# Replacing a list scheduler by a written-out order table in a fused linear-attention and mixture-of-experts kernel

## The chip, the cores and the metric

The kernel runs on one core of a Trainium2 chip. The metric is the device time of one execution in microseconds. The kernel before takes 152.34 us (median of three runs, 151.07 to 153.26).

## What is computed

The first half is a linear attention with a decaying state, for 4 sequences of 768 tokens and 8 heads of 48 channels; the second sends each whole sequence through one of 8 experts, chosen by the mean of the attention's output.

```python
# attention, per sequence b and head h; state is 48x48
for t in range(S):
    y[t]  = r[t] @ (state + outer(u * k[t], v[t]))
    state = w[:, None] * state + outer(k[t], v[t])
# mixture of experts: x = y of all heads side by side, [768, 384]
logits = x.mean(axis=0) @ w_gate            # 8 logits for the sequence
e      = argmax(logits)
out    = softmax(logits)[e] * (relu(x @ w1[e]) @ w2[e])   # 384 -> 1024 -> 384
```

Inputs and outputs are float32; the matrix products of the kernel are in bf16, except the gate's.

## The kernel before

**Blocks.** The 3072 tokens are cut into 12 blocks of 256 tokens (`g`, three to a sequence). A block has two halves of 128 rows, `j` being a half of the partitions and `c` the parity of the token. For each block the kernel

- loads k, r and v (`load`, L71 to L80, 384 KB each, on the sync queue);
- scales k and r by powers of the decay and casts them (`scale`, L362; GpSimd, 1.82 us a piece), and casts v (`prep_v`, L373; ScalarE);
- turns k and r by TensorE (`transposes`, L377, the tile `twp`) and takes them out of PSUM (`evac_t`, the tile `kr`);
- forms products for the bonus term u (`prod`, `bonus`, `bonus_out`, `bonus_v`: tiles `prod`, `tcol`, `vt`);
- multiplies scores k times r in two rounds (`scores`, tile `at`, always the same PSUM bank pair), and masks them on VectorE (`masked`, tile `gt`, 1.22 us);
- multiplies masked scores by v into two banks (`y_mms`), adds the part of the carried state (`inter`) and of the bonus (`add_bonus`, step name `vt y`), and updates the state (`state_mms`, `state_out`, `carried`, PSUM tile `s`);
- casts the result to bf16 (`evac_y`, tile `xn`), adds up its columns for the mean (`pool_mms`), and turns it back to channels by tokens (`turn_back`, `evac_x`, tile `xt`).

**Sequences.** After three blocks come the sum of the pool (`pool_sum`), the gate's logits (`gate`, tile `lgp`), the choice (`choose`, maximum and its index on VectorE), and `weights` (L635): GpSimd reads the expert's number into a register and issues three transfers of that expert's weights, which convert to bf16 on the way. Then follow 16 up-projection steps of three matmuls (`mm1`, tile `hp`), each with a rectified evacuation (`relu`, tile `ht`), and 6 down-projection tiles in two halves of four matmuls each (`mm2`, tile `op`), each with a multiplication by the gate's weight (`gated`, tile `ob`) and then a store.

**Order.** [...] Each piece is a *step* with the engines that may do it and an estimated duration on each, the steps that it needs, the PSUM banks that it uses, and whether it takes or frees one of three rotating banks (`b0` to `b2`). `schedule` (L234) is a list scheduler over these: it keeps an estimated clock per engine, and takes the ready step that could start first, among equals the one with the longest tail of work plus a hand-set lead (`LEAD`, L216). If its estimate leaves TensorE a gap of over 0.35 us it fills it with matmuls on zeros (`fill`, L110), which are there to keep TensorE active.

**Buffers and waits around the change.** The loaded k, r and v have four buffers each (`AHEAD = 4`, L49), so the load of block g waits until block g - 4 has been scaled and cast. From block 6 on (`FENCED = 6`, L847) the loads also stand behind `fence`, a four-byte transfer on the same sync queue that waits for the gate's weight of sequence 0 and comes after the first expert's weights have been issued. The gate's logits take one of the three rotating banks from `gate` to `exp`.

Of the kernel before, what the change touches and what calls it, by code (L numbers as in the profile page):

```python
# [14 lines left out]
ACT = mybir.ActivationFunctionType  # L15


@with_exitstack
def kernel(
# [29 lines left out]
    AHEAD = 4  # L49
# [4 lines left out]
    xpool = ctx.enter_context(tc.tile_pool(name="xpool", bufs=B))  # L54
# [33 lines left out]
    wrow = const.tile([1, DM], FP32, tag="wrow", name="wrow")  # L88
# [17 lines left out]
    nc.sync.dma_start(out=wg, in_=moe_w_gate.rearrange("(p ct) e -> p ct e", p=128))  # L106
# [12 lines left out]
    fill("b0", 5)  # L119
# [24 lines left out]
    lnw = const.tile([128, H, D], FP32, tag="lnw", name="lnw")  # L144
# [51 lines left out]

    class Step:
        def __init__(self, key, on, emit, needs, banks, takes, frees, form, lands):
            self.key, self.on, self.emit, self.needs = key, on, emit, list(needs)
            self.banks, self.takes, self.frees = list(banks), takes, frees  # L200
            self.form, self.lands = form, lands
            self.then, self.tail, self.scale = [], 0.0, 1.0

    steps = {}
    lands = {}

    def step(key, on, emit, needs=(), banks=(), takes=None, frees=None, form=None, data=()):
        assert key not in steps, key
        steps[key] = Step(key, on, emit, [n for n in needs if n is not None], banks, takes,
                          frees, form, list(data))  # L210

    ANY = ("b0", "b1", "b2")
    FORM = 0.1
    RUN = 3
    SCALE0, SCALE = 4.35, 3.77
    LEAD = {  # L216
        "weights": 20.0, "gate sums": 20.0, "gate": 29.7, "choose": 24.1, "mm2": -1.8,
        "r": -2.7, "v": -1.6, "load": 12.4, "mm1": 2.4, "t": 0.5, "tcol": 3.8, "carry": -1.1,
        "relu": -4.2, "late": -1.0, "kr": -2.7, "y": 4.8, "xn": -7.6, "gated": 8.4, "gt": -1.3,
        "vt y": 2.3,  # L220
    }
    names = {"PE": nc.tensor, "DVE": nc.vector, "ACT": nc.scalar, "POOL": nc.gpsimd,
             "SP": nc.sync}

    def lag(src, dst, settled):
        if src == dst:
            return 0.0
        if src == "PE":
            return 0.22
        if dst == "PE":  # L230
            return 0.1 if settled else 0.3
        return 0.15

    def schedule(free, lands_first, chains):  # L234
        lands.update(lands_first)
        for s in steps.values():
            for n in s.needs:
                steps[n].then.append(s.key)
        links = {}
        for chain in chains:  # L240
            for x, y in zip(chain, chain[1:]):
                links.setdefault(x, []).append(y)
        done = set()

        def tail(key):
            stack = [key]
            while stack:
                x = stack[-1]
                if x in done:
                    stack.pop()  # L250
                    continue
                after = steps[x].then + links.get(x, [])
                rest = [y for y in after if y not in done]
                if rest:
                    stack.extend(rest)
                    continue
                s = steps[x]
                s.tail = s.scale * min(s.on.values()) + max(
                    [steps[y].tail for y in after], default=0.0)
                done.add(x)  # L260
                stack.pop()

        for key in steps:
            tail(key)

        end, eng_of = {}, {}
        bank_use = {}
        owner = dict.fromkeys(ANY)
        held = {}
        open_at = dict.fromkeys(ANY, 0.0)  # L270
        form, stream = ["128"], [0.0]
        left = {k: len(s.needs) for k, s in steps.items()}
        ready = [k for k, n in left.items() if n == 0]
        settled = [True]

        def start_on(s, e):
            t = free[e]
            for n in s.needs:
                t = max(t, end[n] + lag(eng_of[n], e, settled[0]))
            for x in s.lands:  # L280
                t = max(t, lands[x])
            for bank in s.banks:
                for other, till in bank_use.get(bank, {}).items():
                    if other != e:
                        t = max(t, till + lag(other, e, settled[0]))
            if s.takes:
                spare = [open_at[x] for x in ANY if owner[x] is None]
                if not spare:
                    return None
                t = max(t, min(spare))  # L290
            return t

        while ready:
            best = {}
            for k in ready:
                s = steps[k]
                if any(x not in lands for x in s.lands):
                    continue
                for e in s.on:
                    t = start_on(s, e)  # L300
                    if t is not None:
                        best.setdefault(e, []).append((t, k))
# [47 lines left out]
            for n in s.then:  # L350
                left[n] -= 1
                if left[n] == 0:
                    ready.append(n)
# [544 lines left out]
```

## Time and profile before

| | us |
|---|---|
| median of three runs | 152.34 |
| span of the profiled execution | 150.4 |
| TensorE busy | 133.4 (89%) |
| VectorE busy | 73.4 (49%) |
| ScalarE busy | 83.8 (56%) |
| GpSimd busy | 67.9 (45%) |
| up-projection matmuls (`hp`), 192 | 35.6 |
| down-projection matmuls (`op`), 192 | 34.7 |
| mask products (`gt`), 24 | 29.2, 1.22 each |
| k and r scalings on GpSimd, 22 | 40.1, 1.82 each |

TensorE's mean granted clock is 0.932 of full. A line of the page's groups gives the source line, the engine, the operation with the program's names for output and input, the number of instructions, busy time and mean of one, and the engine's idle time just before them with what ended it. [...] The chain of work is followed back from the last instruction, at each step to whatever released it. Times in the trace count from the start of the span. Line numbers are those of the kernel before.

### The profile page before, as it was taken

How to read it: one execution, taken by the hardware profiler on the slowest of the kernel's cores; microseconds unless marked ns; L12 is line 12 of the kernel's file. 1: busy time of each engine (PE TensorE's matmuls, PEld its weight loads, DVE VectorE, ACT ScalarE, POOL GpSimd, SP SyncE). 2: the span in 40 equal slices, each digit the busy share in tenths (PEclk: the TensorE clock that was granted, in tenths of full speed). 3: DMA queues.
4: the chain of work that ended last, by engine and by line, in shares of the span. 5: the costliest groups of instructions: out<-in, count | busy, mean ns of one | idle time of the engine just before them, and what ended most of it. 6: DMA issues, size and time to landing. Idle time of an engine off the chain costs nothing.

```text
span 150.4 us, 4471 instructions
## 1 busy us (share of the span) xinstructions
PE 133.4 (89%) x1924; PEld 93.2 (62%) x1926; DVE 73.4 (49%) x157; ACT 83.8 (56%) x148; POOL 67.9 (45%) x59
## 2 busy tenths in 40 slices
PE   6999899599899999980399999999999999699990
PEld 2157678487577756640386767766676676466660
DVE  6569999776854479750359705554502130200000
ACT  0984966335264873400655597655388544499441
POOL 4199399966313999941966901650021006000000
PEclk9999999965599999996559999999999999999999
DMA  2999999202999999999994020099930006995043
GB/s 60 303 325 318 264 278 288 67 4 38 162 201 291 242 300 280 201 216 269 255 331 168 4 105 0 5 136 187 283 134 0 0 4 155 169 264 147 4 189 125
DMA packets 44599, 25.47 MB, mean 169 GB/s; under 512 B 38819, under 2 KB 42148, under 8 KB 44580
## 3 DMA queue, kind: packets, MB, share of 16 engines
q1 hardware_dynamic: 39460, 18.89, 43.9%
q0 software_dynamic: 4288, 6.29, 25.7%
q8 instruction: 15, 0.25, 0.6%
q10 hardware_dynamic: 832, 0.00, 0.3%
q14 instruction: 4, 0.03, 0.1%
HBM read 26.76 MB, written 4.72 MB: 209 GB/s over the span
## 4 chain that ended last, share of the span: by engine, by line
PE 50%; DMA 29%; SPq 7%; issue 3%; ACT 3%; POOL 2%; DVE 2%; POOLq 0%; ACTq 0%
DMA v<-in_v_dram 22%; PE hp L656 17%; PE op L674 14%; SPq L77 6%; DMA w<-in_moe_w_dram 4%; PE twp L381 4%; PE at L409 3%; DMA k<-in_k_dram 3%; PE y L495 3%; ACT kr L369 2%; PE y L473 2%; PE s L523 2%; PE lgp L604 2%; PE y L483 2%; POOL vt L452 1%
## 5 line engine op out<-in xcount | busy, mean ns | idle before, releaser
L656 PE MATMUL hp<-xt,w 128*128 128x384 bf16 x192 | 35.6, 330 | 1.7 <-DMA w<-in_moe_w_dram 1.4
L666 ACT ACTIVATE ht<-hp 128x384 bf16<-128x384 f32 x60 | 29.3, 490 | 11.8 <-PE hp L656 11.6
L674 PE MATMUL op<-w,ht 128*128 128x384 bf16 x192 | 34.7, 326 | 0.0
L421 DVE TENSOR_TENSOR gt<-at,mask 128x1024 bf16<-128x1024 f32 x24 | 29.2, 1218 | 3.4 <-PE at L409 3.1
L452 POOL TENSOR_TENSOR vt<-vb,tcol 128x768 bf16<-128x768 bf16 x11 | 16.2, 1477 | 28.0 <-DVE tcol L447 20.6
L656 PEld LDWEIGHTS <-w 128*128 128x128 bf16 x192 | 20.4, 116 | 10.6 <-DMA w<-in_moe_w_dram 1.6
L674 PEld LDWEIGHTS <-ht 128*128 128x128 bf16 x192 | 17.8, 98 | 10.4
L363 POOL TENSOR_TENSOR kp<-k,dk 128x768 bf16<-128x768 f32 x11 | 20.1, 1830 | 5.5 <-DMA k<-in_k_dram 5.2
L363 POOL TENSOR_TENSOR rp<-r,dr 128x768 bf16<-128x768 f32 x11 | 20.0, 1819 | 5.3 <-DMA r<-in_r_dram 5.3
L685 ACT ACTIVATE ob<-op,gw 128x384 f32<-128x384 f32 x21 | 12.1, 580 | 14.8 <-PE op L674 14.2
L409 PE MATMUL at<-kr 48*64 48x128 bf16 x384 | 11.1, 240 | 9.3 <-ACT kr L369 8.5
L369 ACT COPY kr<-twp 128x1024 bf16<-128x1024 bf16 x14 | 14.1, 1012 | 7.6 <-PE twp L381 7.6
L369 ACT CAST vb<-v 128x768 bf16<-128x768 f32 x11 | 9.2, 833 | 16.2 <-DMA v<-in_v_dram 16.1
L409 PEld LDWEIGHTS <-kr 48*64 48x64 bf16 x384 | 7.4, 116 | 12.9 <-ACT kr L369 9.1
L495 PE MATMUL y<-vb,gt 64*128 64x48 bf16 x384 | 14.2, 185 | 0.2 <-DVE vt L452 0.2
L396 DVE TENSOR_TENSOR prod<-twp,kr 128x512 bf16<-128x512 bf16 x24 | 9.3, 416 | 10.1 <-ACT kr L369 10.0
L495 PEld LDWEIGHTS <-gt 64*128 64x128 bf16 x384 | 11.6, 96 | 4.2 <-issue 3.1
L641 POOL DMA_DIRECT2D w<-in_moe_w_dram x8 | 6.4, 804 | 15.0 <-DVE ssum L627 11.4
L523 PE MATMUL s<-vb,kp 64*128 64x96 bf16 x160 | 11.3, 217 | 0.0
L369 ACT CAST xn<-y 128x384 bf16<-128x384 f32 x18 | 8.1, 484 | 5.4 <-PE y L483 4.3
L381 PE MATMUL twp<-ident,kp 128*128 128x128 bf16 x96 | 10.2, 234 | 0.7 <-remote 0.4
L381 PE MATMUL twp<-ident,rp 128*128 128x128 bf16 x96 | 10.3, 235 | 0.1
(73 smaller groups left out, 148.7 us busy)
## 6 DMA issues: line engine op xcount, KB each, us to landing
k<-in_k_dram SPq DMA_DIRECT2D x12, 384.0 KB, 5.4
r<-in_r_dram SPq DMA_DIRECT2D x12, 384.0 KB, 5.6
v<-in_v_dram SPq DMA_DIRECT2D x12, 384.0 KB, 5.5
out_dram<-ob SPq DMA_DIRECT2D x11, 384.0 KB, 5.3
w<-in_moe_w_dram POOLq DMA_DIRECT2D x8, 384.0 KB, 7.2
w<-in_moe_w_dram POOLq DMA_DIRECT2D x4, 768.0 KB, 12.3
out_dram<-ob SPq DMA_DIRECT2D x2, 192.0 KB, 1.8
wuT<-in_w_dram ACTq DMA_DIRECT2D x2, 0.8 KB, 3.5
```

The lines of the kernel that those rows point to most:

```text
L363: eng.tensor_mul(dst[:, cs, :, 0:D].rearrange("q c h d -> q h c d"), src[:, :, cs, :], dec[:, :, cs, :])
L369: nc.scalar.copy(dst, src)
L381: nc.tensor.transpose(out=twp[:, o + p, :], in_=src[:, c, 2 * p : 2 * p + 2, :].rearrange("s a b -> s (a b)"), identity=ident,)
L409: nc.tensor.matmul(out=at[64 * j : 64 * j + 64, a, pp, cs, :], lhsT=kt[q, p, j, cs, :], rhs=rt[q, p, j].rearrange("q c i -> q (c i)"), sta ...
L421: nc.vector.tensor_mul(gts[g][:, rnd].rearrange("q a p c t -> q (a p) (c t)"), ats.pop((g, rnd)).rearrange("q a p c t -> q (a p) (c t)"), ...
L452: eng.tensor_mul(vts[g], vbs[g].rearrange("q c h d -> q (c h) d"), src.to_broadcast([128, 2 * H, D]))
L495: nc.tensor.matmul(out=yj[:, D * h : D * h + D], lhsT=gt[q, p // 2, a, p % 2, c, :], rhs=vb[q, c, h, :], start=begin(g, j), stop=(c == 1), ...
L523: nc.tensor.matmul(out=sp[:, 96 * p : 96 * p + 96], lhsT=kp[g % NR][qo, c, 2 * p : 2 * p + 2, :].rearrange("s a b -> s (a b)"), rhs=vb[qo, ...
L656: nc.tensor.matmul(out=hp[:, 0:SB], lhsT=w1s[b, ft // 4][:, ct, ft % 4 :: 4], rhs=xts[b][:, ct, SB * sb : SB * sb + SB], start=(ct == 0), ...
L666: nc.scalar.activation(out=o, in_=src, func=ACT.Relu)
L674: nc.tensor.matmul(out=moe_ps[b, si][:, 0:DM], lhsT=hts[b][:, ft, 128 * si : 128 * si + 128], rhs=w2s[b][:, ft, :], start=(ft == 0), stop= ...
L685: nc.scalar.activation(out=ob[:, c, :], in_=src, func=ACT.Copy, scale=gws[b][:, 0:1])
```

## The change

The scheduler, its leads and its estimates are taken out. In their place stands `ORDER`, a table with one entry per step: engine, step, its numbers, and the rotating bank where one is concerned. It was found beforehand by annealing over a model of the kernel's time. `run` walks through it and emits the steps. Seven more things come with it:

- k, r and v get six buffers (`AHEAD = 6`); loads of block g wait for block g - 6, and only blocks from 7 on stand behind the fence (`FENCED = 7`). To make room, `prod` has two buffers, masked scores and bonus products three, turned x three, and the logarithm of the decay shares its tile with the loaded decay row.
- The engine of a step is chosen by the table, and more steps may go to VectorE: scalings of k and r, casts of v, and bonus products.
- The gate's logits go to spare columns of the state's PSUM bank; the next sequence's first state update waits for `exp` of the sequence before instead of its pool sum.
- The order inside each expert (which up-projection tile, which down-projection tile) is free, and layers of different sequences and blocks are interleaved anew.
- The zero matmuls are written in the table: runs of 1, 2, 6, 2 and 3, and eight instead of nine at the start.
- Channels are taken in contiguous groups of 128 instead of every third, for the turned x, the pool, the rows of the gate's and the expert's weights; the turned x of a half stays contiguous instead of being spread over even and odd tokens.
- Accordingly a store becomes two transfers of 64 partitions, one for even and one for odd tokens.

Code for transposes by DMA is added too, but switched off (`T_DMA = 99`, `X_DMA = ()`). The diff, cut to its core:

```diff
+ORDER = """\
+DVE k 0 0; DVE r 0 0; ACT late; fill 1 b0; PE t 0 0 b0; DVE k 0 1; DVE r 0 1; J k 0; J r 0
+POOL r 1; fill 2 b1; PE t 0 1 b1; ACT kr 0 1; ACT v 0; DVE kr 0 0; fill 6 b2; PE at 0 0; DVE k 1
...
+DVE tcol 3; DVE xt 1 b0; DVE gt 3 1; PE inter 2 0; ACT xn 2 0; PE t 4 1 b1; PE pool 1; PE pool 2
+DVE gate_sums 0; PE t 4 0 b2; PE gate 0; ACT kr 4 1; ACT kr 4 0; DVE k 5; DVE choose 0
+POOL vt 3; POOL r 5; POOL weights 0; ACT exp 0; fill 3 b0; PE at 4 0; DVE prod 4 0 b2
+DVE prod 4 1 b1; DVE gt 4 0; POOL v 5; PE turn 2 b0; PE t 5 0 b2; ACT xt 2 b0; ACT kr 5 0
+PE s 3 0; PE t 5 1 b1; ACT kr 5 1; DVE st 3 1; PE at 4 1; PE bonus 4; PE s 3 1; PE vt_y 3
+PE inter 3 1; DVE gt 4 1; DVE st 4 0; DVE tcol 4; PE at 5 0; ACT xn 3 0; ACT xn 3 1
+DVE prod 5 0 b2; DVE prod 5 1 b1; PE inter 4 0; PE carry 4; PE s 4 0; PE bonus 5
+PE mm1 0 2 0 b0; PE mm1 0 3 0 b2; ACT relu 0 2 0 b0; PE mm1 0 2 1 b1; ACT relu 0 3 0 b2
...
+PE mm1 0 6 1 b1; DVE relu 0 1 0 b2; DVE gt 6 0; SP fence; SP load 7; SP load 8; SP load 9
+PE mm1 0 7 1 b0; PE mm1 0 5 0 b2; DVE relu 0 7 1 b0; DVE r 7; ACT relu 0 6 1 b1
+ACT relu 0 5 0 b2; POOL vt 5; POOL k 7; POOL r 8; PE mm1 0 4 1 b1; PE inter 5 1; PE s 5 1
+PE at 6 1; PE vt_y 5; ACT v 6; ACT relu 0 4 1 b1; POOL k 9; DVE xn 5 1; PE mm1 0 7 0 b2
...
+DVE gate_sums 3; PE mm1 2 6 0 b0; PE gate 3; DVE choose 3; ACT relu 2 4 1 b2; ACT relu 2 6 0 b0
+ACT relu 2 4 0 b1; SP store 1 1; SP store 1 0; SP store 1 2; POOL weights 3; PE turn 10 b2
...
+PE mm2 3 1 0 b0; PE mm2 3 0 0 b1; PE mm2 3 2 0 b2; PE mm2 3 2 1; PE mm2 3 0 1; ACT gated 3 2 b2
+SP store 3 1; PE mm2 3 1 1; DVE gated 3 0 b1; ACT gated 3 1 b0; SP store 3 0"""
...
-    AHEAD = 4
+    AHEAD = 6
...
-    fill("b0", 5)
+    fill("b0", 4)
...
-    def schedule(free, lands_first, chains):
+    def run(order):
...
+            s.emit(names[eng], bank) if bank else s.emit(names[eng])
...
-    def gate(b, bank):
-        lgp = pp_any.tile([128, 512], FP32, tag=bank, name=f"lgp{b}")
+    def gate(b):
+        lgp = s_ps[b][:, TC + 2 * H : TC + 2 * H + E]
...
-        dst = out[b, L * gi : L * gi + L, :].rearrange("(q c) m -> q c m", c=2)
-        nc.sync.dma_start(out=dst[:, cs, :], in_=obs[b, gi][:, cs, :])
+        dst = out[b, L * gi : L * gi + L, :].rearrange("(j i c) m -> c i j m", j=2, c=2)
+        for c in range(2):
+            nc.sync.dma_start(out=dst[c][:, cs, :], in_=obs[b, gi][64 * c : 64 * c + 64, cs, :])
...
-                 [("k", g - NR), ("r", g - NR), ("v", g - NR)]
+                 [(x, g - AHEAD) for x in "krv" if g >= AHEAD]
...
-                step((x, g), {"POOL": 1.82},
+                step((x, g), {"POOL": 1.82, "DVE": 1.1},
...
-                       ("gate sums", b - 1) if gi == 0 and b else None]
+                       ("exp", b - 1) if gi == 0 and b else None]
...
-    FENCED = 6
+    FENCED = 7
+    T_DMA = 99
+    X_DMA = ()
...
-    schedule({"PE": 6.8, "DVE": 6.0, "ACT": 7.6, "POOL": 8.2, "SP": 6.0}, first, [jobs])
+    run(ORDER)
```

In the table `t` is `transposes`, `at` is `scores`, `gt` is `masked`, `s` is the state update with half of y, `st` is `state_out`, `turn` is `turn_back`, `xt` is `evac_x`; the first number is the block, or the sequence for `gate`, `weights`, `mm1`, `relu`, `mm2`, `gated` and `store`.

## The prediction

> **What bounds the kernel now.** I read the page's 40 slices first, then busy time by stretches, then the chain of work that ended last in order of time, then the wait table and the sync queue's timeline. The slices, each 3.76 us long, for TensorE, its granted clock and DMA:
>
> ```profile
> PE   6999899599899999980399999999999999699990
> ...
> PEclk9999999965599999996559999999999999999999
> DMA  2999999202999999999994020099930006995043
> ```
>
> TensorE is nearly always busy, so the time is its work plus its losses. The losses are the two dips in the clock (slices 9 to 11 and 19 to 21), the hole at slices 18 and 19, and a small one at slice 35. Busy time of each engine over the stretches that I cut there (start:end, length, then PE, PEld, DVE, ACT, POOL, granted clock, DMA share, GB/s):
>
> ```profile
> 28.30:31.40 3.10, 1.34 (x48) 1.05 (x46) 1.77 (x5) 2.44 (x3) 3.10 (x3) 1.00 0.00 0
> 31.40:41.60 10.20, 9.76 (x154) 7.61 (x155) 7.58 (x16) 3.36 (x5) 4.90 (x5) 0.51 0.56 80
> ...
> 66.90:73.70 6.80, 0.05 (x1) 0.00 (x0) 0.02 (x1) 1.79 (x3) 2.92 (x2) 0.66 1.03 248
> 73.70:79.50 5.80, 5.80 (x120) 5.15 (x120) 4.17 (x7) 3.25 (x5) 3.87 (x3) 0.52 1.12 330
> ```
>
> 1.8 us idle, then 10.2 us at half clock; later 6.8 us idle, then 5.8 us at half clock. At half clock 16 score matmuls start over 0.57 us against 0.35, 8 transposes take 0.85 against 0.45: 1.6 to 1.9 times as long. So the spells lose some 10.2 x 0.41 = 4 us and 5.8 x 0.41 = 2.4 us. The chain names what ended the hole and what stands at the end (start, length, what):
>
> ```profile
> 57.60 14.23 DMA v<-in_v_dram
> 71.91 0.04 ACT vb L369
> 71.95 0.70 issue
> 72.65 1.01 ACT kr L369
> 73.66 0.04 issue
> 73.70 0.64 PE at L409 x12
> ...
> 86.04 3.90 PE hp L656 x24
> ...
> 124.60 6.54 DMA w<-in_moe_w_dram
> 131.14 0.05 issue
> 131.19 7.99 PE hp L656 x48
> 139.18 7.81 PE op L674 x48
> 147.01 0.58 ACT ob L685
> ```
>
> A load of v (block 9) took 14.2 us where the page's median is 5.5. ScalarE casts v before it evacuates the transposes of block 8 (`kr`), because its queue is in that order, and TensorE's scores stood behind that. The wait table says the same (total, times, longest), and the sync queue shows that issuing itself was held back after it:
>
> ```profile
> ACT vb L369 <- DMA v<-in_v_dram: 16.1, 7, 9.9
> ...
> PEld L409 <- ACT kr L369: 9.1, 2, 7.1
> ```
>
> ```profile
> 60.06 7.33 SPq L77 DMA_DIRECT2D k<-in_k_dram  x1
> ```
>
> Expert 1's weights had been issued at 56.3 us, so both streams shared the DMA engines. The same cast order makes the first gap: at 28.6 us ScalarE waits 2.3 us for v of block 5 while `kr` of block 4 stands behind it, and the gate matmuls stand behind block 4's scores.
>
> [...]
>
> **The change, part by part.**
>
> *TensorE's work.* The real matmuls are the same in number. From the warm rows of the chain: an up-projection step (3 matmuls) 0.49, a down-projection half (4) 0.65, 8 transposes 0.45, 16 scores 0.35, 16 y with 8 state matmuls 0.50, `inter` 0.17, bonus `vt y` 0.29, `turn` 0.34, `gate` 0.58, bonus column 0.18, carry 0.16, pool 0.14. From the first up-projection of the new table to its end: experts 64 x 0.49 + 48 x 0.65 = 62.6; transposes 12 x 0.45 = 5.4; scores 13 x 0.35 = 4.6; y and state 15 x 0.5 = 7.5; inter 15 x 0.17 = 2.6; vt y 8 x 0.29 = 2.3; turn 9 x 0.34 = 3.1; gate 3 x 0.58 = 1.7; pool, bonus, carry 3.1. Sum 92.9 us. As a check, the same sum in before from its first up-projection (41.0 us) to the last matmul (147.0) is about 92, and 106 passed: 6.8 hole, 2.4 and 0.3 at half clock, 1.4 waiting for expert 3, leaving 3 us of small waits. I carry 3 us over (2 to 5).
>
> *Up to the first gate.* VectorE had 18.3 of 20.3 us busy from 8.0 to 28.3. Its queue up to the first sum of the pool holds 20.3 us of issue-to-issue time before, 20.9 after (block 1's k scaling comes to it at two halves of 0.557 us, two evacuations leave it). It starts at 6.1, so the sum falls near 28 in both. The first gate, however, no longer stands behind block 4's scores; it sits right after block 4's transposes. In before the sum was done at 28.2 and gate matmuls began at 31.3: now about 28.4. VectorE then scales k of block 5 (1.05) before `choose` (0.55): 29.8. GpSimd finishes r of block 5 near 30.2 and then needs 1.2 us for the expert number (123.4 to 124.6 in before): weights issue at about 31.3 instead of 34.6. Before, the first up-projection ran 6.4 us after issue; 5.4 is the shortest landing in the trace, 8.3 the median. I take 6.5: 37.8 (36.7 to 39.6).
>
> *Clock before the experts.* Between gate and first up-projection the table gives TensorE about 6 us of work, three of the zero matmuls among it (0.66), for some 9.4 us. That is 65% busy, where the 3.1 us that led to the first spell were 43% busy. It may stay warm (cost 0) or fall as before (cost 4.0). I take 1.5, nearer to warm. The other zero matmuls of the table (11 x 0.22 = 2.4 us) lie ahead of block 2 and hide behind VectorE.
>
> *Loads with six buffers.* Blocks 4, 5 and now 6 are loaded without a fence and without waiting for a buffer of four blocks back. Blocks 7, 8 and 9 follow the fence, which waits for the gate weight; VectorE reaches that after 9.5 us more of its queue, near 38.5 (36.2 before). Nine loads at the 1.3 us at which the queue issues them are 12 us, with some 3 us of weights left over: landed by about 54. GpSimd scales k of block 9 before it issues expert 1's weights, so the two cannot collide as at 57.6. TensorE wants block 7 after 16 up-projections and 5 us of other work, 37.8 + 13 = 51, and its k and r, first of the nine, land some 5 us before; block 9 is wanted at about 60. So the 6.8 us hole and its 2.4 us at half clock go. v of block 9 goes to GpSimd, which also frees ScalarE's queue. Loads of 10 and 11 stand behind store 0 1, are wanted some 15 us later, and hide under expert 1.
>
> *Expert 3's wait.* From gate 3 the up-projection needs 122.8 to 131.2 = 8.4 us in before. The new table has a whole second layer (12 x 0.65), two turns and one up-projection step, 9.0 us, in that time. The 1.4 us go.
>
> *Moved to VectorE.* Its queue grows from 69 to about 94 us (7 whole scalings, 2 bonus products, a cast, 15 more activations, 10 more gated outputs, 3 more casts of y), ScalarE's and GpSimd's shrink. In the stretch of expert 0 VectorE has 13.7 us for TensorE's 14.6; elsewhere 75 to 80%. Nothing extra beyond the 3 us.
>
> *The gate's logits in the state bank* free one of three rotating banks for about 2 us per sequence, and make the next sequence's state wait for `exp`, which has run by then. The changed layouts (turned x in contiguous blocks, expert rows) keep counts and element numbers. Zero for both.
>
> *The end.* From the last matmul 3.4 us passed. Now the last store is 384 KB in two transfers of 192 KB instead of one of 192: at the 1.2 us that a 384 KB load takes of the queue, 0.6 more, at most the difference of the landing rows, 5.3 - 1.8 = 3.5. I take 0.8: 4.2.
>
> Sum: 37.8 + 92.9 + 3.0 + 1.5 + 4.2 = 139.4 us of span. The median run was 1.9 over the profiled span, the profiled run 1.6; with 1.8: **141.2 us**.
>
> **Rivals.**
> *A hole stays* (0.17). A load or an expert's weights come late, because the fence is 2 us later and every queue is now fixed in an order that cannot answer. For it: loads of 13 and 14 us in the trace. Against: 4 us or more of slack at blocks 7 to 9. 141.2 + 6.8 = 148.0.
> *VectorE or the handoffs become the bound* (0.08). If TensorE stands once per block for a mask product (1.22 us, the costliest VectorE row), 12 x 1.22 = 14.6 more: 155.8, slower. For it: 94% VectorE load around expert 0[...]. Against: outside that stretch it has 20% free.
> *Everything hides* (0.15). Warm throughout, 1 us of small waits, tail 4.0: 37.8 + 92.9 + 1 + 4.0 + 1.8 = 137.5.
>
> **How the numbers follow.** Forecast 0.60. With all unknowns at their low ends 36.7 + 92.9 + 2 + 0 + 4.0 + 1.8 = 137.4; at their high ends 39.6 + 92.9 + 5 + 4 + 5.5 + 1.8 = 148.8. The range 136 to 149 takes in the fast rival and most of the hole. Faster means under 149.3, slower over 155.4. Faster: 0.60 + 0.15 + 0.15 of the hole; slower 0.07; between 0.03.
>
> **What would show it.** First gate near 28.4 and first expert matmul near 38; no TensorE gap over 2 us between 45 and 125; weights 1 issued after block 9's loads landed; no wait before expert 3; clock at full from 48 on. Wrong if TensorE shows many waits of 0.3 to 1 us on VectorE, if the clock falls again after the gate for 10 us, or if the casts of v still hold `kr`.

## The result, and the profile after

The changed kernel takes 138.09 us (median of four runs, 138.05 to 141.46) against 152.8 us for the kernel before (151.07 to 153.86): a ratio of 0.9065, 95% interval 0.8981 to 0.9148. Forecast were 141.2 us, range 136 to 149.

All lines of "after" below are of a second profile of the same kernel (138.13 us, span 136.5), since the first is of a run of 141.46 us, one of the three among its ten executions on record that took 141.17 to 141.77 us, at a mean clock of 0.980 to 0.982, where the other seven took 137.38 to 138.13 us at 0.989 to 0.996.

The 40 slices of the changed kernel, 3.41 us each, for TensorE, its granted clock and DMA:

```profile
PE   6999999999899999999999999999999999999940
...
PEclk9999999999999999999999999999999999999996
DMA  2999999995999999599289972992008379970354
```

In this profile both dips of the clock and the hole have gone; the last digit of the clock stands behind the last matmul. The same in numbers, for the first two stretches cut as before and for 41.6 to 80 us, where the hole was (start:end, length, then PE, PEld, DVE, ACT, POOL, granted clock, DMA share, GB/s):

```profile
28.30:31.40 3.10, 3.05 (x56) 2.38 (x55) 3.07 (x9) 2.65 (x5) 3.10 (x2) 1.00 0.89 236
31.40:41.60 10.20, 9.53 (x228) 7.19 (x226) 9.31 (x17) 6.53 (x10) 8.65 (x8) 1.00 0.97 173
41.60:60.00 18.40, 18.40 (x281) 13.62 (x278) 16.31 (x29) 11.82 (x21) 7.71 (x6) 1.00 0.97 228
60.00:80.00 20.00, 20.00 (x368) 14.82 (x366) 15.63 (x29) 11.26 (x23) 7.99 (x5) 1.00 0.91 222
```

From 41.6 to 80 TensorE is never idle. In the 3.1 us that led to the first spell it now has 3.05 us busy instead of 1.34, and in the next 10.2 us it starts 228 matmuls at full clock where it started 154 at half. The chain that ended last has no load of k, r or v left in it, and one transfer of weights (start, length, what):

```profile
29.59 1.71 POOL rp L333
31.76 0.60 issue
32.39 4.99 DMA w<-in_moe_w_dram
37.42 2.14 PE hp L669 x12
...
125.31 5.86 PE op L688 x36
131.24 0.58 ACT ob L699
```

From 8 us to its last matmul TensorE has no wait over 0.3 us but the one for these weights, 0.39 us in TensorE's timeline (the bracket at the end is the idle time before the group, and what ended it):

```profile
37.42 2.14 PE L669 MATMUL hp<-xt,w 128*128 128x384 bf16 x12 [0.39 <-DMA w<-in_moe_w_dram]
```

The ledger between the profiled spans, 150.4 and 136.5, has three entries. The first expert matmul starts at 37.4 instead of 41.0: -3.6. From there to the last matmul pass 93.7 us (37.4 to 131.2) instead of 106.0: -12.3. From the last matmul to the end pass 5.3 us instead of 3.4: +1.9. The sum is -14.0; the spans differ by 13.9.

The middle entry is the big one. Of its 12.3 us, before had 6.8 in the hole, 2.4 (an estimate of the prediction) at half clock behind it, 0.3 of the first spell that reached past 41 us, and 1.4 waiting for expert 3: 10.9. The remaining 1.4 us are only in small part idle time: TensorE is busy for 97.4 of the 106.0 us in before, so that besides the hole and expert 3's wait it is idle for 0.4, and for 93.7 of the 93.7 us in the kernel after. Where the last 1.0 us come from is not shown.

### The profile page after: what moved, and what is told of

It is laid out like the page before. It is cut to its first block, busy times and chain, and to the rows that moved or that the text cites. A ratio compares the mean times of both kernels' runs of the same rounds, so it can differ in the third digit from the quotient of the medians.

```text
span 139.8 us, 4473 instructions
## 1 busy us (share of the span) xinstructions
PE 129.2 (92%) x1928; PEld 89.4 (64%) x1928; DVE 98.5 (70%) x193; ACT 67.6 (48%) x119; POOL 55.2 (39%) x52
## 4 chain that ended last, share of the span: by engine, by line
PE 65%; SPq 15%; DMA 10%; DVE 3%; issue 2%; POOL 1%; ACT 0%; POOLq 0%; ACTq 0%
PE op L688 23%; PE hp L669 22%; SPq L176 14%; DMA w<-in_moe_w_dram 5%; DMA r<-in_r_dram 5%; PE twp L351 4%; PE y L498 3%; PE xp L582 2%; PE at L402 2%; PE s L526 2%; PE y L468 2%; PE y L486 1%; DVE rp L333 1%; PE s L616 1%; SPq L206 1%
## 5 line engine op out<-in xcount | busy, mean ns | idle before, releaser
L669 PE MATMUL hp<-xt,w 128*128 128x384 bf16 x192 | 37.8, 338 | 2.0 <-DMA w<-in_moe_w_dram 2.0
L680 ACT ACTIVATE ht<-hp 128x384 bf16<-128x384 f32 x45 | 21.5, 490 | 34.0 <-PE hp L669 34.0
L669 PEld LDWEIGHTS <-w 128*128 128x128 bf16 x192 | 20.2, 115 | 10.9 <-DMA w<-in_moe_w_dram 2.0
L333 POOL TENSOR_TENSOR kp<-k,dk 128x768 bf16<-128x768 f32 x8 | 14.7, 1841 | 15.6 <-DMA k<-in_k_dram 15.6
L446 POOL TENSOR_TENSOR vt<-vb,tcol 128x768 bf16<-128x768 bf16 x9 | 14.0, 1551 | 16.3 <-DVE tcol L441 11.5
L339 ACT COPY kr<-twp 128x1024 bf16<-128x1024 bf16 x16 | 16.0, 1014 | 6.9 <-PE twp L351 6.9
L333 POOL TENSOR_TENSOR rp<-r,dr 128x768 bf16<-128x768 f32 x7 | 12.7, 1818 | 5.9 <-DMA r<-in_r_dram 5.8
L701 DVE TENSOR_SCALAR ob<-op,gw 128x384 f32<-128x384 f32 x13 | 7.9, 615 | 9.5 <-PE op L688 9.4
L498 PE MATMUL y<-vb,gt 64*128 64x48 bf16 x384 | 14.4, 180 | 0.2
L682 DVE TENSOR_SCALAR ht<-hp 128x384 bf16<-128x384 f32 x19 | 10.2, 554 | 5.4 <-PE hp L669 5.3
L699 ACT ACTIVATE ob<-op,gw 128x384 f32<-128x384 f32 x11 | 6.4, 581 | 14.3 <-PE op L688 14.3
L526 PE MATMUL s<-vb,kp 64*128 64x96 bf16 x160 | 10.2, 204 | 0.0
L402 PE MATMUL at<-kr 48*64 48x128 bf16 x384 | 9.9, 220 | 0.3 <-DVE gt L415 0.2
```

Of the source, the lines that this page charges most:

```text
L333: eng.tensor_mul(dst[:, cs, :, 0:D].rearrange("q c h d -> q h c d"), src[:, :, cs, :], dec[:, :, cs, :])
L339: nc.scalar.copy(dst, src)
L402: nc.tensor.matmul(out=at[64 * j : 64 * j + 64, a, pp, cs, :].rearrange("q (c i) -> q c i", c=2), lhsT=kt[q, p, j, cs, :], rhs=rt[q, p, j] ...
L446: eng.tensor_mul(vts[g], vbs[g].rearrange("q c h d -> q (c h) d"), src.to_broadcast([128, 2 * H, D]))
L498: nc.tensor.matmul(out=yj[:, D * h : D * h + D], lhsT=gt[q, p // 2, a, p % 2, c, :], rhs=vb[q, c, h, :], start=begin(g, j), stop=(c == 1), ...
L526: nc.tensor.matmul(out=sp[:, 96 * p : 96 * p + 96], lhsT=kp[g % NR][qo, c, 2 * p : 2 * p + 2, :].rearrange("s a b -> s (a b)"), rhs=vb[qo, ...
```

## Experiments

Each kernel was timed in three rounds beside the kernel before, whose median was 152.2 to 152.9 us in all of them; medians below are in us. A first group changes the kernel after, a second the kernel before. For the second, the order that the scheduler had made was written out as a table, so that one entry could be moved at a time and all else stayed.

### The kernel after once more

No edit.

> The changed kernel once more, to read its undisturbed profile. The first profile of it shows a spell of 3.4 us at half clock right after the wait for expert 0's weights (39 to 43 us). Theory (clock): the three undisturbed runs, 138.05 to 138.13 us with a mean clock of 0.99, have no such spell or a shorter one: 138.1 us, clock in the stretch 39 to 43 at or near 1.0. Rival (the 3 us come from elsewhere, such as transfers): the spell is there at 138.1 us too.

Measured: 137.99 (137.38 to 141.77), ratio 0.9056 (0.8954 to 0.9158). In this profile (138.13 us) the clock is full from 11.2 us, where the trace's record of it begins, to the last matmul. So the spell is not in every execution, as the theory had it. Three of the ten executions have a mean clock that would fit such a spell, and one of these was profiled. There TensorE waits 1.95 us for expert 0's weights, here 0.39. The stretch with the long wait, the first line below, is 43% busy, and half clock follows it.

That is a pattern in all fourteen profiles of this record. In those of before and of the run of 141.46 us the clock record begins at 7.64 and 8.53 us, and up to the last matmul the clock changes only at whole multiples of 3.41 us from there: it is at half from 31.53 to 41.77 and from 69.08 to 79.32 in before, and from 39.25 to 42.67 in the other. Cut each profile into stretches of this length, counted from the beginning of its clock record to the last matmul. There are 11 stretches at full clock in which TensorE is busy for 1.88 us or less, and half clock follows each; it follows none of the 479 with 1.90 us or more. The two nearest to the boundary are the second line, from "The three together" below (half clock followed), and the third, from "The kernel before with its casts of v later" (it did not):

```profile
35.84:39.25 3.41, 1.46 (x39) 1.03 (x37) 3.41 (x5) 0.00 (x0) 2.59 (x2) 1.00 1.22 209
```

```profile
35.35:38.76 3.41, 1.88 (x53) 1.27 (x49) 3.12 (x7) 0.80 (x1) 1.59 (x2) 1.00 1.07 146
```

```profile
65.29:68.70 3.41, 1.90 (x28) 0.87 (x26) 2.93 (x5) 0.18 (x1) 0.59 (x1) 1.00 1.10 263
```

### The zero matmuls of the table

```diff
-DVE k 0 0; DVE r 0 0; ACT late; fill 1 b0; PE t 0 0 b0; ...
+DVE k 0 0; DVE r 0 0; ACT late; PE t 0 0 b0; ...
```

and so for all five runs of them, 14 zero matmuls; those ahead of the first transposes stay.

> The changed kernel without the 14 matmuls on zeros that the table writes (the 8 ahead of the first transposes stay). Theory: 11 of them lie where TensorE waits for VectorE and cost nothing when taken away; the three after the first gate keep TensorE 72% busy before expert 0's weights land, so without them the clock falls more often or longer: 138 to 143 us. Rival (they only fill gaps): 138.1, no difference, clock as before; or up to 0.6 faster if they stood on the path.

Measured: 144.05 (143.65 to 146.06), ratio 0.9468 (0.9361 to 0.9574): 6.1 us lost by leaving work out. TensorE and its clock in the slices of this kernel (3.56 us each):

```profile
PE   6968999998778999999999999999999999999950
...
PEclk9996555599999999999999999999999999999998
```

The clock falls near 12 us and stays at half until 29. The stretch of 8 to 29 us and its start, first of the kernel without them, then of the kernel after (columns as above):

```profile
8.00:10.00 2.00, 0.61 (x7) 0.37 (x6) 1.94 (x4) 1.98 (x5) 0.92 (x1) 1.00 1.16 320
10.00:12.00 2.00, 1.41 (x29) 1.04 (x29) 1.65 (x2) 1.06 (x2) 1.64 (x2) 0.92 1.17 321
12.00:29.00 17.00, 17.00 (x276) 13.34 (x274) 11.49 (x18) 7.73 (x10) 12.85 (x9) 0.51 1.02 272
```

```profile
8.00:29.00 21.00, 20.48 (x437) 15.11 (x437) 18.40 (x30) 13.86 (x22) 17.78 (x11) 1.00 1.07 283
```

From 8 to 12 us TensorE has 2 us busy of 4, and then runs 17 us at half clock, although it is busy in all of these 17. The first gate begins at 33.60 instead of 29.46, the first expert matmul at 43.19 instead of 37.42, behind three waits of 0.5 to 1.3 us, and the last matmul comes 5.9 us later. In the kernel after the record of the clock begins only at 11.2 us in this profile, but at 8.5 in the other, and both show full clock from there until past 37. So the fall came behind a stretch in which TensorE was busy for half of the time. What lifts the clock again is not shown: here TensorE was busy for all of the 17 us at half, and in before for 9.8 of the 10.2 us of the first spell.

The forecast of 138 to 143 us was missed, and the three fills behind the gate were not the ones that mattered: the spell lies ahead of them, and the clock is full from 29 us to the last matmul without them. The fills are not quite free, since the first scores begin at 10.03 us without them and at 10.9 and 12.0 in the two profiles with them, but they hold the clock, which the prediction's working gave no value. One thing stays open: of the four executions without fills the one that took 146.06 us has a mean clock of 0.995, which leaves no room for such a spell, and it was not profiled.

### More zero matmuls

```diff
-PE mm1 0 2 0 b0; PE mm1 0 3 0 b2; ACT relu 0 2 0 b0
+fill 8 b0; PE mm1 0 2 0 b0; PE mm1 0 3 0 b2; ACT relu 0 2 0 b0
```

> The changed kernel with 8 more matmuls on zeros (1.8 us) in the 2.0 us in which TensorE waits for the first expert's weights. Theory (clock): [...]the spell at half clock after 39 us is gone in every run: 138.1 or up to 1 less, never 141. Rival (the wait is too short to matter, the clock falls for another reason): as often 141 as without them.

Measured: 138.97 (138.68 to 139.34), ratio 0.9139 (0.906 to 0.9218). The first up-projection starts at 38.38 instead of 37.42, and the median is 1.0 longer, where the theory had no cost. No run of it was longer than 139.34, and its mean clock was 0.994 or more in all four. Eight more fills ahead of expert 0 cost a microsecond in each execution and, as far as four show, take away the spell: their mean is 139.0 us, and so is that of the ten executions of the kernel after. On the whole they bring nothing.

### Four load buffers under the table

```diff
-    AHEAD = 6
+    AHEAD = 4
-SP load 5; SP load 6; fill 2 b1; ... ACT v 1; POOL vt 1
+fill 2 b1; ... ACT v 1; SP load 5; POOL vt 1
-POOL v 2; POOL vt 2; ...
+POOL v 2; SP load 6; POOL vt 2; ...
```

> The changed kernel with four load buffers instead of six; the loads of blocks 5 and 6 move down in the sync queue behind the casts that free their buffers, all else as in the table. Theory (the table's order does most): blocks 7 to 9 still load right behind the fence, with a wait for buffers of 1 to 3 us; 138 to 141 us. Rival (six buffers are what removes the hole): TensorE waits 5 us or more between 45 and 70 us, 143 to 149 us.

Measured: 137.82 (137.69 to 137.94), ratio 0.9146 (0.909 to 0.9203), the time of the kernel after. TensorE starts expert 0 at 37.06, behind a wait of 0.46 us, and has no longer gap. Under the table the six buffers bring nothing: loads 5 and 6 are still issued ahead of the fence and well before they are wanted.

### The gate's logits back in a rotating bank

```diff
-PE gate 0; ... ACT exp 0
+PE gate 0 b0; ... ACT exp 0 b0
```

with b2, b2, b1 for the next three; `exp` 1, `exp` 3 and one `relu` come earlier, as the banks then require.

> The changed kernel with the gate's logits in one of the three rotating banks again (b0, b2, b2 and b1), held from the gate to exp; three evacuations or exps are moved up in the table so that a bank is free in time. The three zero matmuls after gate 0 then wait for exp 0. Theory: each gate costs TensorE about 0.5 us of waiting for a bank: 139 to 141 us. Rival (the bank was never short): 138 us.

Measured: 142.99 (141.09 to 144.39), ratio 0.9519 (0.943 to 0.9607), 5.0 us over the kernel after. The profile is of the shortest run, 141.09 us, with the clock full throughout. TensorE's groups with the longest idle times before them:

```profile
30.47 0.81 PE L211 MATMUL fill<-zero 128*128 128x512 bf16 x2 [0.92 <-ACT exps L633]
...
53.88 1.46 PE L685 MATMUL op<-w,ht 128*128 128x384 bf16 x8 [0.92 <-ACT exps L633]
...
81.81 0.83 PE L614 MATMUL lgp<-wg,pooled 128*128 128x8 f32 x6 [0.94 <-ACT xt L337]
...
109.38 0.49 PE L580 MATMUL xp<-ident,xn 128*128 128x128 bf16 x6 [1.27 <-ACT ht L677]
```

Four waits, one per sequence, together 4.05 us: TensorE stands for a bank that the logits hold, or that is emptied late because of them (at 109.38 the evacuation stands behind `exp` 3 in ScalarE's queue). The waits had been expected at 0.5 us each. They cover the 3.0 us by which this run is longer; the other executions took 1.8 to 3.3 us more, at mean clocks of 0.982 to 0.985, and were not profiled. The prediction priced this edit at zero. The table was found for the other placement, so this is its price within this table; a table found for rotating banks might lose less.

### Seven scalings back on GpSimd

```diff
-DVE k 1 ... DVE k 5 ... DVE r 6 ... DVE r 7 ... DVE k 8 ... DVE r 9 ... DVE r 10
+POOL k 1 ... POOL k 5 ... POOL r 6 ... POOL r 7 ... POOL k 8 ... POOL r 9 ... POOL r 10
```

> The changed kernel with seven whole scalings (k 1, k 5, r 6, r 7, k 8, r 9, r 10) back on GpSimd, at the same places of the table. Theory (the moves pay: k 5 on GpSimd stands ahead of r 5 and the weights of expert 0, 1.8 us, and k and r of blocks 6 to 10 come 1.8 us later each): 140 to 142, first expert matmul at about 39.2. Rival 1 (they pay nothing, since GpSimd is 41% busy and VectorE's two scalings beside GpSimd took 1.9 us instead of 0.95): 137.5 to 138.6. Rival 2 (worse than before: TensorE waits for scalings at each block from 6 to 10): 145 or more.

Measured: 144.24 (143.85 to 145.83), ratio 0.9486 (0.9393 to 0.9579), 6.2 us over the kernel after, although GpSimd is only 47% busy. TensorE's groups with the longest waits, and then the stretch behind the last of these:

```profile
12.88 0.40 PE L349 MATMUL twp<-ident,kp 128*128 128x128 bf16 x4 [1.17 <-POOL kp L331]
33.67 0.40 PE L349 MATMUL twp<-ident,rp 128*128 128x128 bf16 x4 [1.26 <-POOL rp L331]
41.85 0.40 PE L349 MATMUL twp<-ident,rp 128*128 128x128 bf16 x4 [0.79 <-POOL rp L331]
80.14 0.40 PE L349 MATMUL twp<-ident,rp 128*128 128x128 bf16 x4 [1.63 <-POOL rp L331]
```

```profile
81.00:85.00 4.00, 4.00 (x58) 2.81 (x57) 1.25 (x3) 2.01 (x5) 1.62 (x1) 0.57 0.62 181
```

Expert 0 starts at 38.70, 1.3 later; TensorE waits for scalings at four places, 4.85 us in all; and the last wait is followed by a spell at a mean clock of 0.57. The time lies between the theory's 140 to 142 us and the second rival's 145 or more. So the moves to VectorE are worth some 6 us, again at the table's own places. The rows of the kernel after give the reason: VectorE scales a k in 1.05 us on average (three of them) where GpSimd needs 1.82 (eight), and with two engines on them k and r of a block can be scaled side by side (k of block 5 from 29.28 us on VectorE, r from 29.55 on GpSimd) instead of one after the other.

### The end

Three kernels bear on the end. The first splits the last store in two, each half stored as soon as it is there:

```diff
-DVE gated 3 0 b1; ACT gated 3 1 b0; SP store 3 0
+DVE gated 3 0 b1; SP store 3 0 0; ACT gated 3 1 b0; SP store 3 0 1
```

> The changed kernel with the last store (384 KB after the last two evacuations) split so that the first half leaves after the first of them, as the kernel before does. The profile shows 5.3 us from the last matmul to the end where before had 3.4. Theory: the size of the last store sets the tail, so 1 to 1.9 us go: 136.2 to 137.1. Rival: the tail is set by the 13 stores that stand in the queue before it or by the finish of a transfer whatever its size: 138.1.

Measured: 138.58 (137.74 to 141.33), ratio 0.9119 (0.9017 to 0.9222): no gain, against the theory; its profile ends 5.8 us after its last matmul. The second issues the last store's second transfer from ScalarE's queue:

```diff
-        for c in range(2):
-            nc.sync.dma_start(...)
+        for c, e in enumerate((nc.sync, nc.scalar if (b, gi) == (B - 1, 0) else nc.sync)):
+            e.dma_start(...)
```

> The changed kernel with the second half of its last store issued from ScalarE's queue instead of behind the first half in the sync queue. Theory (the end is long because the 384 KB go out in pieces of 1.5 KB from 64 partitions at 130 to 290 GB/s, whichever queue issues them): 137.5 to 138.4, the tail stays at 5 to 5.8 us. Rival (the second issue, held up behind the first in one queue, is the end): tail 4.6, 137.3 or less.

Measured: 137.9 (137.66 to 138.07), ratio 0.9031 (0.896 to 0.9101): the same as the kernel after, span 136.4 against 136.5. The second issue does not set the end. What does is seen in the last microseconds. The columns are as above; first before, where the last matmul ended at 147.0, then after, where it ended at 131.2:

```profile
146.00:147.00 1.00, 0.98 (x7) 0.39 (x4) 0.00 (x0) 0.34 (x1) 0.00 (x0) 1.00 0.82 329
147.00:148.00 1.00, 0.00 (x0) 0.00 (x0) 0.00 (x0) 0.58 (x1) 0.00 (x0) 1.00 0.53 197
148.00:149.00 1.00, 0.00 (x0) 0.00 (x0) 0.00 (x0) 0.00 (x0) 0.00 (x0) 1.00 0.51 194
```

```profile
131.00:132.00 1.00, 0.16 (x1) 0.00 (x0) 0.16 (x1) 0.58 (x1) 0.00 (x0) 1.00 0.18 46
132.00:133.00 1.00, 0.00 (x0) 0.00 (x0) 0.00 (x0) 0.00 (x0) 0.00 (x0) 1.00 0.95 246
133.00:134.00 1.00, 0.00 (x0) 0.00 (x0) 0.00 (x0) 0.00 (x0) 0.00 (x0) 1.00 0.97 260
134.00:135.00 1.00, 0.00 (x0) 0.00 (x0) 0.00 (x0) 0.00 (x0) 0.00 (x0) 0.54 0.71 235
```

Before has 0.39 MB to move in the two microseconds after its last matmul, with the DMA engines half busy. After has 0.79 MB from 131 on: the last two stores, 384 KB each, of which the first is issued at 130.5 and the second at 131.9, and the engines are 95 to 97% busy for two microseconds. Splitting or issuing elsewhere leaves these bytes to move: with the second issue on ScalarE's queue the two microseconds from 132 on show 246 and 250 GB/s, with the engines 95 to 99% busy. The form of the stores changed too: before, the stores ahead of the last two were in pieces of 3 KB from 128 partitions, after, all are in pieces of 1.5 KB from 64. What the form adds to the bytes was not tried, and neither was a table whose last two stores lie further apart.

### The kernel before with six buffers

```diff
-    AHEAD = 4
+    AHEAD = 6
-    FENCED = 6
+    FENCED = 7
```

and loads 5 and 6 behind load 4, ahead of the fence; a few other buffers are smaller to make room.

> The kernel before with its own order of work (every engine's instructions as the list scheduler left them), but six load buffers, blocks 4 to 6 loaded ahead of the fence, and the other buffers shrunk as in the change (2 of prod, 3 of gt, vt and xt). Theory (late loads made the hole, and the buffers held them back): block 9's v lands well before 67 us, the 6.8 us hole and the half clock after it (2.4) go, the first gap (1.8 and its half clock, 4.0) stays since the order is the same: 143 to 145 us. Rival (the order of the queues made the hole, buffers are secondary): at most 2 us go, 150 to 153 us.

Measured: 147.8 (144.91 to 148.79), ratio 0.968 (0.9544 to 0.9816), 4 to 5 us gained, with an interval of 2.8 to 6.9: between the theory (143 to 145 us) and the rival (150 to 153). In the profile, of a run of 148.75 us, TensorE's hole is shorter but there, and the sync queue still shows the stall:

```profile
71.32 0.42 PE L524 MATMUL at<-kr 48*64 48x128 bf16 x16 [3.98 <-ACT kr L484]
```

```profile
57.09 7.71 SPq L174 DMA_DIRECT2D k<-in_k_dram  x1
```

So with three loads fewer behind the fence the stall at expert 1's weights stays as long as it was (7.33).

### The kernel before with its casts of v later

```diff
-ACT v 5; ... ACT kr 5 1; ... ACT v 9; ... ACT kr 8 0
+... ACT kr 5 1; ACT v 5; ... ACT kr 8 0; ACT v 9
```

> The kernel before with its own order and four buffers; only two casts of v on ScalarE are moved back: that of block 5 behind the evacuations of blocks 4 and 5, that of block 9 behind the first evacuation of block 8. Theory (the casts held kr, and kr held TensorE): the 1.8 us gap at 28.6 us and its half clock (4.0) go, and the hole at 67 us shrinks to about 3 us, because the transposes of block 9 then wait for r of block 9, which is scaled at 72.6: 143 to 147 us. Rival (loads arrive late whatever ScalarE does): the time moves by under 2 us.

Measured: 149.69 (148.01 to 151.76), ratio 0.9898 (0.9855 to 0.9941), 1.6 us by the ratio (0.9 to 2.2), less than the theory's 143 to 147. The profile is of the shortest of twelve runs, 148.01 us. The first gap shrinks from 1.75 to 0.51 us, but by itself that brings nothing: TensorE then waits 1.93 us for expert 0's weights, half clock follows, and at 46.7 us it has reached the same matmul as before. The hole does not go. TensorE only gets a few steps further, and then stands for 3.69 us for the next thing that waits behind the same cast on ScalarE; the stall is unchanged:

```profile
70.88 0.33 PE L586 MATMUL y<-st,kr 128*128 128x96 bf16 x4 [3.69 <-ACT xn L482]
```

```profile
57.16 7.54 SPq L172 DMA_DIRECT2D k<-in_k_dram  x1
```

### The kernel before with expert 1's weights later

```diff
-POOL k 7; ... POOL r 7; ... POOL weights 1; ... POOL k 8
+POOL k 7; ... POOL r 7; ... POOL k 8; ... POOL r 9; POOL weights 1
```

This moves one entry of the table, and GpSimd issues the weights at 65.7 us instead of 56.3, right behind its scaling of r of block 9 (63.9 to 65.8), as the table has it. In before, TensorE began with expert 1 at 86.0 us, so they have the time.

> The kernel before with its own order written out, and one thing moved: the issue of expert 1's weights goes from behind r 7 to behind r 9 in GpSimd's queue. Theory (the loads behind the fence and expert 1's weights collide on the DMA engines, and this makes v of block 9 take 14.2 us): v of block 9 lands some 6 us after its issue at 57.6, the hole of 6.8 us and the 2.4 us at half clock behind it go: 152.3 - 9.2 = 143 (142 to 145.5), and the weights, issued at about 66, are there before expert 1 begins at 79. Rival 1 (the loads are late by their own number, or because of the cast of v ahead of kr): the hole stays at 3 us or more, 148 to 152. Rival 2 (the collision only moves): the weights of expert 1 now meet the loads of blocks 10 and 11, TensorE waits there instead, 146 to 150.

Measured: 144.37 (142.49 to 145.01), ratio 0.9419 (0.9321 to 0.9516): 8.5 us from moving three transfers in one queue, within the theory's 142 to 145.5. In the profile (145.01 us) the stall is gone, the slices (3.59 us each) show neither the hole nor the second dip, and between 60 and 80 us TensorE is busy for 19.6 us, in before for 13.2. The sync queue at v of block 9 and k of block 10, GpSimd's queue at the weights, and TensorE, its clock and the stretch from the slices and the windows:

```profile
58.30 2.14 SPq L172 DMA_DIRECT2D v<-in_v_dram  x1
60.54 1.22 SPq L172 DMA_DIRECT2D k<-in_k_dram  x1
```

```profile
65.69 1.58 POOL L754 DMA_DIRECT2D w<-in_moe_w_dram  x2
```

```profile
PE   6999899929989998999998999999999999599990
...
PEclk9999999995559999999999999999999999999998
```

```profile
60.00:80.00 20.00, 19.55 (x386) 13.91 (x385) 16.48 (x28) 11.06 (x17) 16.24 (x12) 1.00 1.11 259
```

The first rival expected 148 to 152 and the second 146 to 150, and both are out. Now v of block 9 lands 6.0 us after its issue. What made it take 14.2 us, and with it the hole, was the issue of expert 1's weights in the middle of the loads. The second rival is right in that the collision moves: r and v of block 11, issued at 65.5 and 68.1 beside the weights, now take 14.4 and 13.1 us to land, but TensorE does not stand for them. The packets in the trace of before show how the two streams share the DMA engines: from 52 to 58 us, without weights under way, the loads moved 300 GB/s; from 60 to 68 us they moved 42 GB/s and took 0.22 of the time of the 16 engines, and the weights 165 GB/s and 0.92. The first dip of the clock stays, since nothing ahead of 41 us was touched.

### The three together

Six buffers, the casts and the weights, all in the order of before.

> The kernel before with its own order written out and three edits at once: six load buffers with loads 5 and 6 ahead of the fence, the casts of v 5 and v 9 behind the evacuations that they held up, and expert 1's weights behind r 9. Other buffers are smaller so that it fits. Theory (the three are most of what the table gains outside the clock before expert 0 and the gate's logits): no hole, first gap of 1.8 us gone, about 142 (140.5 to 144), 1 us under the kernel with the weights moved alone. Rival (each of them only moves the wait): not under 145.

Measured: 142.42 (141.74 to 143.65), ratio 0.9317 (0.9241 to 0.9393): within the theory's 140.5 to 144, and 2 us under the weights alone, a difference that the two intervals do not separate, where the other two bring some 5 and 1.6 us by themselves. So the gains overlap, as all three work on the same hole. In the profile (143.65 us) expert 0 starts at 39.27, behind a wait for weights, and the clock is at half for 6.8 us from 38.8 on:

```profile
39.27 1.15 PE L771 MATMUL hp<-xt,w 128*128 128x384 bf16 x3 [1.71 <-DMA w<-in_moe_w_dram]
```

```profile
38.00:60.00 22.00, 20.37 (x253) 13.98 (x254) 10.63 (x25) 12.11 (x22) 14.12 (x9) 0.84 1.09 263
```

To the kernel after 4.4 us are missing by the medians, and 5.5 by the spans of the two profiles, 141.9 and 136.5. The start of expert 0 gives 1.9 of the 5.5, the half clock an estimated 6.8 x 0.41 = 2.8; the end, which is shorter in this kernel, takes 1.9 back. The remaining 2.7 are not traced singly; gaps of TensorE over 0.2 us behind that start come to 1.2.

## Why the prediction was right

The time was forecast within 3.1 us and for the reason given, the hole and its spell; the terms of the sum compare like this, in us:

| term | forecast | kernel after |
|---|---|---|
| first expert matmul | 37.8 (36.7 to 39.6) | 37.4 |
| TensorE's work up to the last matmul | 92.9 | with the waits 93.7 |
| small waits | 3.0 (2 to 5) | 0.8, as what is left |
| half clock | 1.5 (0 to 4) | 0 in this profile |
| the end | 4.2 (4.0 to 5.5) | 5.3 |
| time over span | 1.8 | 1.6 |

**Up to the first gate.** Forecast 28.4, measured 29.46 (the `L616` group in TensorE's timeline). The weights were issued at 32.4 instead of 31.3: r of block 5, ahead of them in GpSimd's queue, ended at 32.1 instead of 30.2, since it began later and took 2.53 us instead of 1.82, while VectorE scaled k of the same block. The landing was quicker, 5.0 us instead of 6.5. That the two misses cancel is luck. That the gate's earlier place makes the earlier start is read from the traces; no run moved it back.

**The clock before the experts.** A part chance of a spell was carried at 1.5 us, and a part chance it is: the profile of 138.13 us has none, as the rival "everything hides" said, and that of 141.46 has 3.4 us at half clock behind the wait for expert 0's weights. The median falls on the side without it. The profiles of the kernels with the other two ends, with four buffers, with more fills, and with the logits in rotating banks have none; with the scalings on GpSimd there is one, but at 81 us.

**Loads.** The mechanism is right, and the moved weights show it. The prediction said that loads and expert 1's weights cannot collide since GpSimd scales k of block 9 before it issues these. The queues of the kernel after, sync first, then GpSimd:

```profile
40.55 0.70 SPq L888 DMA_DIRECT2D fence<-gw  x1
...
42.40 1.50 SPq L176 DMA_DIRECT2D v<-in_v_dram  x1
...
51.31 1.09 SPq L176 DMA_DIRECT2D v<-in_v_dram  x1
...
68.53 0.54 SPq L176 DMA_DIRECT2D k<-in_k_dram  x1
```

```profile
53.78 1.81 POOL L333 TENSOR_TENSOR kp<-k,dk 128x768 bf16<-128x768 f32 x1 [0.96 <-PE s L616]
55.53 1.58 POOL L654 DMA_DIRECT2D w<-in_moe_w_dram  x2
```

The last load of the nine is issued at 51.3, k of block 9 scaled by 55.6, the weights issued right behind it, and the next loads come 13 us after. That v of block 9 lands only at 57.1, 1.5 us behind the first of the weights, hurt nothing. The fence is 2 us later than forecast, which cost nothing. The same separation holds at the first expert: in before v of block 6 was issued at 38.4, just behind the weights of expert 0, and held for 7.68 us; here the fence comes 5.7 us after those weights, and v of block 7 takes 1.50.

One attribution under that heading was wrong: the title "Loads with six buffers" and the sentence on blocks 4, 5 and 6 give the buffers a part in it. In the order of before they are worth 4 to 5 us, but under the table four buffers give 137.82. Under the table it is the order of the transfers that removes the hole, not the room for them.

**Expert 3's wait.** It is gone, as forecast.

**Moved to VectorE.** "Nothing extra" was right for the cost: VectorE is 71% busy and TensorE waits nowhere for it over 0.3 us. But the step asked only what the moves cost, not what they save, and the run with the scalings back on GpSimd puts that at 6 us. Nor did it count what the two engines cost each other. In the kernel after, VectorE's scaling of r of block 6 took 2.23 us while GpSimd formed a bonus product; those of blocks 7 and 9 took 0.95, with GpSimd idle or issuing:

```profile
37.47 2.23 DVE L333 TENSOR_TENSOR rp<-r,dr 128x768 bf16<-128x768 f32 x1
```

```profile
37.40 1.47 POOL L446 TENSOR_TENSOR vt<-vb,tcol 128x768 bf16<-128x768 bf16 x1
```

**The gate's logits.** "Zero for both" fell for the first of the two edits: in this table their place is worth 5.0 us. The changed layouts were not tried alone.

**The end.** This term was mis-sized by 1.1 us, 5.3 instead of 4.2. The step looked at the issue of the last store (0.6 more). The run with that issue on another queue shows that it costs nothing, and the trace that the bytes of the last two stores queue up for the DMA engines. How much the new form of the stores adds is open.

The error of 3.1 us is the sum of the terms: -0.4 for the start, -2.2 for small waits (with the work as forecast), -1.5 for the clock, +1.1 for the end, -0.2 for the time over the span, which is -3.2. Small waits were carried over from before at the same size, and that is the largest miss. In before they were what was left of a sum, and TensorE's idle time there shows only 0.4 us of them, so nothing spoke for finding 3 us again. What keeps TensorE supplied are, among others, the two edits that were priced at zero, the logits' bank and the moves to VectorE, and the fills: taking any one of the three away costs 5 to 6 us.

## What to carry to other kernels

When a load takes several times its usual time (here 14.2 us, and 6.0 with the weights moved), look first for the other stream that was issued in the same microseconds; moving that one issue, if its consumer has time, can be worth more than more buffers. An edit that adds no work and takes none away still needs a price for what it frees (a bank, a queue, a clock that stays up): ask what would wait if it were undone. At the end of a kernel count the bytes that are still to be stored when the last matmul ends, and not only the transfers.

## What the runs showed of the hardware

- In the fourteen profiles half clock followed each of the 11 stretches of 3.41 us in which TensorE, at full clock, was busy for 1.88 us or less, and none of the 479 with 1.90 us or more. No idle time of that whole length was needed: in five of the 11 the longest wait was 1.6 to 2.0 us (before 1.75, after at 141.46 us 1.95, later casts 1.93, the three together 1.71, scalings on GpSimd 1.63).
- Without the table's zero matmuls two thin stretches of 2 us (TensorE busy 0.61 and 1.41 us, from 8 to 12 us) were followed by 17 us at half clock, in which TensorE was busy throughout. With eight of them in these 4 us it was busy for 1.94 and 1.59 us (after, 141.46 us), and the clock was full from 8.5 to 39.3 us.
- Issuing a load on the sync queue took 7.33, 7.71 and 7.54 us instead of 1.1 to 1.3 in three profiles (before, six buffers, later casts) where expert weights that GpSimd had issued were under way, and 1.22 us at the same place once these were moved. Not every such issue was held: the last two loads beside the moved weights took 2.4 and 1.1 us to issue, but 14.4 and 13.1 us to land.
- Four times between 27 and 90 us in the kernel after (138.13 us) scalings or bonus products of VectorE and GpSimd overlapped by more than 0.7 us, and one or both were drawn out: a scaling of r on VectorE took 2.23 us instead of 0.95 beside a bonus product on GpSimd of 1.47, as without company; one on GpSimd 2.53 instead of 1.82 beside a k of 1.12 on VectorE; a bonus product on VectorE 1.69 instead of 0.95 beside a k of 1.81 on GpSimd; and a scaling of r on VectorE 1.54, with a k of 1.82 and then a bonus product of 2.19 on GpSimd.
- The last stores, in pieces of 1.5 KB from 64 partitions, moved at 235 to 260 GB/s with the DMA engines 71 to 97% busy; before, with pieces of 3 KB from 128 partitions, 329 GB/s came at 82%. Which of the two differences matters was not tried.
- In the profile of before matmuls overlap: one of the up-projection is listed with 0.33 us in the mean, but 48 of them take 7.99 us in the chain, 0.17 each.
